# A second norm from three sums, and one uneven load, at the end of a cached attention decode

## The chip, the cores and the metric

The kernel runs on one core of a Trainium2 chip. Its engines are TensorE (PE: matmuls, and PEld: its weight loads), VectorE (DVE), ScalarE (ACT), GpSimd (POOL) and SyncE (SP, which issues nearly all transfers); sixteen DMA engines move the data. The metric is the device time of one execution in microseconds, and the number that counts is the median over the runs. Everything is float32.

## The reference

Batch B = 4, one token each, D = 512; 32 query heads in 8 groups of 4, head size 128, 4096 cached positions; a mixer with F = 1792.

```python
mod = (silu(c) @ w_mod).reshape(4, 6, 1, 512)
sa, ca, ga, sb, cb, gb = (mod[:, i] for i in range(6))
h = layernorm(x) * (1 + ca) + sa
x = x + ga * attention(h, k_cache, v_cache, wq, wo)   # softmax over 4096 positions
h = layernorm(x) * (1 + cb) + sb
# the mixer has a LayerNorm of its own:
n = layernorm(h)                                       # eps 1e-5
x = x + gb * (gelu(n[..., None] * w1 + b1) @ w2 + b2)  # per channel, over F
```

The key and value caches are 4 x 8 x 4096 x 128 each, 134 MB together, and every byte is read once. So a row of the result (one of the batch of four) passes three norms: of x, of the sum x1 after the attention (the first one here), and of h, the modulated first one (the "second norm" of the title).

## The kernel before, in words

**Loads.** A pair i (0 to 31) is one batch row and one key/value group. The data come in slots of 32 KB per partition, three in a ring (pool `ring`, tag `kv`). `load_pair(i)` fills one slot with the keys of pair i+2 (16 KB of each of the 128 rows) and the values of pair i (the other 16 KB). All issues go through SP's queue in program order; an issue waits until PE has read the slot's former content. The last pairs are loaded in pieces (LK, LV, LW in the plan), the last values in pieces down to 128 KB.

**Work on a pair.** `scores` (PE, L231), the row maximum (DVE, L236), its turn and spread over the partitions (L240 to L256), `expo` (ACT, L261), the transposition of p (DVE, L267 or L271), `values` (PE, L291; narrow form L303), a copy (L314), the choice of the four heads (L328), the product with wo (L343) and its addition (L361). For pairs 0 to 23 these steps stand in one loop (line 618). Pairs 24 to 31 follow `PLAN` (line 667), an order written out by hand: each word is one step, and each engine works through its own steps in that order.

**Rows and the mixer.** When the eight pairs of a batch row are done, `Mixer` forms x1, its norm, h and the norm of h, then u = gelu(n w1 + b1) in seven pairs of columns (`expand` on DVE L442, `gelu` on ACT L506) and the contraction with w2 (`contract_wide`, PE L453). Channels stand as four blocks of 128 on the partitions, each value eightfold. Rows 0 to 2 do this beside the loads of later rows. Row 2's last two pairs of columns are contracted (`c c` in the plan) and folded (`zc`, line 520, with fold_groups L366) in the last line of the plan.

**The last row** has nothing left to hide behind. Its products with wo go into `pgx` by L348; `tally_up` (L601) and `mean_last` (L604) give the mean of x1 while they run. Then, in the plan's last line: `zs`, squares of x1 - mean with their sum (ACT L741); `za`, a = (x1 - mean)(1 + cb) (DVE L410); `zx`, a copy of x1 (L747); `zq`, the sum of squares over the row (PE L737), from which `zm` makes the deviation sd (ACT L416), h1 = sb sd + a (DVE L417), an epsilon column (L419) and the statistics of h1 (L378, L380); `zb0` and `zb1`, h1 spread over the partitions (PE L427); `zv`, the statistics gathered (L479); `zn`, the aggregate (DVE L396), the inverse root (POOL L100), two ACT copies of h1 less its mean into hb (L436), and wr = -w1 times the inverse root (POOL L437). `T2` and `T3` load ACT's tables for Sqrt and Gelu. `finish` (line 552) then forms the gelus (ACT L557 twice, L562 five times), the contraction (L447), the products with gb (L567 to L577) and the stores.

Of the kernel before, what the change touches and what calls it, by code (L numbers as in the profile page):

```python
# [8 lines left out]
F32 = mybir.dt.float32  # L9
# [15 lines left out]
NARROW = NS - 3  # L25


@with_exitstack
def adaln_decode(ctx: ExitStack, tc: tile.TileContext, small, x, wmod, wq, kk, kv, vv, wo, out):
# [144 lines left out]
    def load_pair(i):  # L174
        t = slots()
        nc.sync.dma_start(t, kv[i])
        key(t[:, 0], i + 2)
        value(t[:, 1], i)
# [194 lines left out]
    XK = cst.tile([P, B, P], F32, name="xk")  # L373
# [34 lines left out]
    def centre(x, mu):  # L408
        a = wk.tile([P, P], F32, name="a")
        dv.scalar_tensor_tensor(a, x, mu, prep[:, 3], op0=OP.add, op1=OP.mult)  # L410
        return a

    def adaln_last(b, pst, a):
        r = cst.tile([P, 1], F32, name="sd")
        h1 = wk.tile([P, P], F32, name="h1")
        nc.scalar.activation(r, pst, AF.Sqrt, bias=epsc, scale=1.0 / D)  # L416
        dv.scalar_tensor_tensor(h1, prep[:, 2], r, a, op0=OP.mult, op1=OP.add)  # L417
        pst = ps_m.tile([P, 27], F32, name="pst", tag="m")
        dv.tensor_scalar(pst[:, 24:27], eps9, r, r, op0=OP.mult, op1=OP.mult)  # L419
        return h1, stats(h1, b), pst  # L420

# [28 lines left out]
    def contract_wide(py, u, js):  # L450
        for e, j in enumerate(js):
            q = j % 4
            mm(py[32 * q:32 * q + 32, :], w2[:, j:j + 1].to_broadcast([P, 32]), u[:, e, :],  # L453
               start=(j < 4), stop=(j >= NF - 4))

    class Mixer:


        def __init__(self, b):
            self.b, self.wide, self.n = b, b < B - 1, 0  # L460
            self.raw, self.done, self.ripe, self.pbs = [], [], 0, []
            self.pst = None
# [15 lines left out]
        def gather_more(self):  # L478
            mm(self.pst[:, 0:24], ones, self.st.rearrange("p a b -> p (a b)"), start=True, stop=True)  # L479
            self.st = self.pst  # L480

        def modulate(self):
            if self.b < B - 1:
                self.h1, self.st = adaln(self.b, self.st)
            else:
                self.h1, self.st, self.pst = adaln_last(self.b, self.st, self.a)
# [26 lines left out]
        def consume(self, most=9):  # L513
            if self.py is None:
                self.py = ps_e.tile([P, D if self.wide else P], F32, name="py", tag="e")
            for u, js in self.done[:most]:
                (contract_wide if self.wide else contract)(self.py, u, js)
            del self.done[:most]

        def gather_up(self):  # L520
            yw = wk.tile([P, D], F32, name="yw", tag="yw", bufs=1)
            dv.tensor_copy(yw, self.py)
            self.py = fold_groups(ps_e, yw, "e")

# [27 lines left out]
    def finish(b, pg, py, hb, wr):  # L552
        uu = ring.tile([P, 16, D], F32, name="uu", tag="kv")
        for js in ((0,), (1,), (2, 3, 4), (5, 6, 7), (8, 9, 10), (11, 12), (13,)):
            j = js[0]
            if j < 2:
                nc.scalar.activation(uu[:, j], hb, AF.Gelu_apprx_tanh, bias=b1[:, j:j + 1], scale=wr[:, j:j + 1])  # L557
                u = uu[:, j:j + 1]
            else:
                u = uu[:, j:j + len(js)]  # L560
                expand(u, hb, wr, js)
                nc.scalar.activation(u, u, AF.Gelu_apprx_tanh)  # L562
# [5 lines left out]
        dv.tensor_add(osb[:, :B - 1], osb[:, :B - 1], XK[:, :B - 1])  # L568
# [28 lines left out]
    mu = cst.tile([P, 1], F32, name="mu")  # L597

# [19 lines left out]
    for i in range(NS - HKV):  # L618
# [43 lines left out]
    mix, row = Mixer(B - 2), Mixer(B - 1)  # L662
# [11 lines left out]
    v30.1 A29 LW p29 f v30.2 v30.3 t31.0 P29 g V30 Y y a30 A30 p30 E x v31.0 f v31.1 v31.2 v31.3 V31 z31 a31 I A31 j p31  # L674
    g T2 zs za zx zq c c zm zb0 T3 zv zb1 zw0 zn zc
# [5 lines left out]
           "N": mix.normalise, "g": mix.gelu, "c": lambda: mix.consume(1), "zc": mix.gather_up, "zv": row.gather_more,  # L681
           "zg": row.gather,
           "zm": row.modulate, "zn": lambda: row.normalise(cst.tile([P, 1], F32, name="yl"))}
    for step in PLAN.split():
# [49 lines left out]
        elif op == "zq":  # L734
            ph = ps_s.tile([P, 8, P], F32, name="ph3", tag="s")
            row.st = ph[:, 2, 0:1]
            mm(row.st, g32[:, 8 * (B - 1):8 * (B - 1) + 1].to_broadcast([P, P]), sq, start=True, stop=True)  # L737
        elif op == "zs":
            sq = cst.tile([P, 1], F32, name="sq")
            flat = wk.tile([P, P], F32, name="flat")  # L740
            nc.scalar.activation(flat, pgx[:, 4], AF.Square, bias=mu, accum_out=sq)  # L741
        elif op == "j":
            tally_up()
        elif op == "za":
            row.a = centre(pgx[:, 4], mu)
        elif op == "zx":
            dv.tensor_copy(XK[:, B - 1], pgx[:, 4])  # L747
        elif op == "zw":
            modmm(pgx[:, 0], 5, (0,))
        elif op == "zb":  # L750
            if i:
                py = ps_v.tile([P, 4, P], F32, name="py3", tag="pv")
            row.spread(py[:, 2:4] if i else ph[:, 4:6], (2 * i, 2 * i + 1))
    finish(B - 1, pgx[:, 0], py[:, 0], row.hb, row.wr)
# [34 lines left out]
```

## Time and profile before

| what | value |
|---|---|
| runs | 386.43, 386.49, 388.0 us; median 386.49 |
| span of the profiled execution | 384.7 us (no other time is recorded for it; the median of the runs is 1.8 above) |
| DMA queue of SP | 7376 packets, 157.33 MB, 95.4% of sixteen engines' span |
| PE, DVE, ACT, POOL busy | 298.7, 198.2, 112.2, 7.7 us |
| last product into pgx, first gelu of the last row, last store issued: starts | 369.25, 373.88, 382.27 us |

Times in rows of the profile count from the span's start. A row of the timeline gives start and duration, the engine and line, out<-in with shapes, how many instructions are merged, and in brackets the engine's idle time before it with what ended it. The DMA share is the mean busy share of sixteen engines. A transfer has landed when the last of its engines is done.

### The profile page before, as it was taken

The page shows a single profiled execution, that of the slowest core. Times are in us where ns is not written, and L with a number is a line of the kernel's source. Part 1 is how long each engine was busy: PE and PEld are TensorE (multiplying, and loading weights), DVE is VectorE, ACT ScalarE, POOL GpSimd, SP SyncE. Part 2 cuts the span into 40 slices and gives each one's busy share as a digit, 9 for nine tenths or more (in the row PEclk, how much of TensorE's full clock was granted, in tenths as well). Part 3 has the DMA queues.
Part 4 walks back from the last instruction along what each step waited for, and adds up shares of the span by engine and source line. Part 5 has one row for each costly group of instructions (what it writes and reads, how often), then busy time and mean ns, then how long its engine had stood idle before and what let it go on. Part 6 is the DMA issues. An engine that isn't in the chain of part 4 may idle for free.

```text
span 384.7 us, 5604 instructions
## 1 busy us (share of the span) xinstructions
PE 298.7 (78%) x2380; PEld 117.2 (30%) x2380; DVE 198.2 (52%) x407; ACT 112.2 (29%) x144; POOL 7.7 (2%) x33
## 2 busy tenths in 40 slices
PE   0856777866966949979877878788888887999984
PEld 0112122311323313334322222342222343333653
DVE  1130251620451424664866545557665567778757
ACT  1001111121110110212567311124575105657276
POOL 1100000000000000000000000000000000000000
PEclk9989555985695685998999998999999999999999
DMA  8999999999999999999999999999999999999930
GB/s 331 433 433 436 411 453 433 409 432 436 423 441 433 434 436 436 434 436 431 429 425 433 428 433 434 429 433 431 429 434 436 434 436 432 424 417 423 418 122 3
DMA packets 7409, 157.69 MB, mean 410 GB/s; under 512 B 964, under 2 KB 1236, under 8 KB 1496
## 3 DMA queue, kind: packets, MB, share of 16 engines
q1 hardware_dynamic: 7376, 157.33, 95.4%
q8 instruction: 18, 0.29, 0.3%
q14 instruction: 7, 0.06, 0.0%
q10 hardware_dynamic: 8, 0.00, 0.0%
HBM read 157.32 MB, written 0.01 MB: 409 GB/s over the span
## 4 chain that ended last, share of the span: by engine, by line
DMA 60%; PE 29%; DVE 7%; ACT 2%; issue 1%; POOL 0%; SPq 0%; POOLq 0%; DVEq 0%
DMA kv<-in_kv 58%; PE s L231 8%; PE pv L291 7%; PE s L122 2%; PE qs L138 2%; DVE m L236 2%; DVE p L267 2%; DMA sm<-in_small 2%; PE pa L343 2%; PE pt L328 2%; ACT uu L562 1%; PE pb L251 1%; PE pve L303 1%; PE pm L240 1%; PE pgx L348 1%
## 5 line engine op out<-in xcount | busy, mean ns | idle before, releaser
L231 PE MATMUL s<-kv,QT 128*32 128x512 f32 x512 | 75.2, 714 | 38.9 <-DMA kv<-in_kv 37.0
L236 DVE TENSOR_REDUCE m<-s 128x1 f32<-128x1024 f32 x32 | 39.2, 1224 | 96.0 <-PE s L231 95.9
L261 ACT ACTIVATE p<-s,nm 128x1024 f32<-128x1024 f32 x32 | 35.7, 1115 | 180.6 <-DVE nm L256 180.5
L291 PE MATMUL pv<-kv,p 128*32 128x512 f32 x464 | 69.8, 670 | 0.7 <-DMA kv<-in_kv 0.7
L231 PEld LDWEIGHTS s<-kv,QT 128*32 128x32 f32 x512 | 15.8, 123 | 84.0 <-DMA kv<-in_kv 52.5
L328 PEld LDWEIGHTS pt<-g,po 128*128 128x128 f32 x236 | 31.1, 205 | 27.2 <-issue 19.9
L343 PE MATMUL pa<-wo,oT 128*32 128x512 f32 x240 | 34.6, 648 | 4.6 <-DVE oT L335 4.4
L328 PE MATMUL pt<-g,po 128*128 128x4 f32 (+2 forms) x236 | 33.9, 267 | 1.5 <-DVE po L314 1.0
L267 DVE STREAM_TRANSPOSE p<-p 128x1024 f32<-128x1024 f32 x25 | 30.9, 1234 | 0.0
L314 DVE COPY po<-pv 128x512 f32<-128x512 f32 x29 | 20.0, 688 | 16.8 <-PE pv L291 16.7
L245 DVE TENSOR_REDUCE mx<-pm 1x128 f32<-1x512 f32 x32 | 21.3, 669 | 1.1 <-PE pm L240 1.1
L442 DVE TENSOR_SCALAR u<-hb,wr,sm 128x512 f32<-128x512 f32 x40 | 19.9, 541 | 1.9 <-POOL wr L437 1.0
L506 ACT ACTIVATE u<-u 128x1024 f32<-128x1024 f32 x20 | 20.4, 1051 | 1.5 <-DVE u L442 1.4
L361 DVE TENSOR_TENSOR acc<-acc,pa 128x512 f32<-128x512 f32 x26 | 17.8, 686 | 4.3 <-PE pa L343 4.2
L261 ACT ACT_TABLE_LOAD x11 | 14.1, 1283 | 20.3 <-DVE nm L256 20.2
L251 PEld LDWEIGHTS pb<-neg,mx 1*128 1x128 f32 x64 | 10.4, 202 | 28.2 <-DVE mx L245 26.5
L122 PE MATMUL s<-wm,sT 128*4 128x512 f32 x16 | 9.1, 732 | 10.6 <-DVE sT L108 10.6
L506 ACT ACT_TABLE_LOAD x13 | 16.7, 1283 | 0.2
L291 PEld LDWEIGHTS pv<-kv,p 128*32 128x32 f32 x464 | 13.4, 146 | 7.2 <-issue 3.1
L240 PE MATMUL pm<-ident,m 128*1 128x128 f32 x32 | 9.3, 289 | 7.4 <-DVE m L236 3.5
L251 PE MATMUL pb<-neg,mx 1*128 1x1 f32 x64 | 13.1, 271 | 2.1 <-DVE mx L245 2.1
L453 PE MATMUL py<-u,sm 128*32 128x512 f32 x80 | 14.4, 616 | 0.0
(158 smaller groups left out, 214.7 us busy)
## 6 DMA issues: line engine op xcount, KB each, us to landing
kv<-in_kv SPq DMA_DIRECT2D x28, 4096.0 KB, 21.9
wq<-in_wq SPq DMA_DIRECT2D x2, 4096.0 KB, 16.3
wo<-in_wo SPq DMA_DIRECT2D x4, 2048.0 KB
kv<-in_kv SPq DMA_DIRECT2D x4, 2048.0 KB, 20.3
wm<-in_wmod SPq DMA_DIRECT2D x2, 2048.0 KB, 14.8
kv<-in_kk SPq DMA_DIRECT2D x1, 4096.0 KB
kv<-in_vv SPq DMA_DIRECT2D x3, 1024.0 KB
wm<-in_wmod SPq DMA_DIRECT2D x1, 1024.0 KB
```

The costliest lines, as they stand in the source:

```text
L231: mm(s[32 * c:32 * c + 32, n * 512:(n + 1) * 512], QT[:, b, h, :], KT[i][:, (n * 4 + c) * 512:(n * 4 + c + 1) * 512], start=True, stop=True)
L236: dv.tensor_reduce(M[i], S[i], axis=AX.X, op=OP.max)
L245: dv.tensor_reduce(mx, M[i].rearrange("o (c r) -> o r c", c=4).unsqueeze(1).to_broadcast([1, 4, 32, 4]), axis=AX.X, op=OP.max)
L251: mm(pb, M[i].rearrange("o c r -> o (c r)"), neg1, start=True, stop=True)
L261: nc.scalar.activation(p, S[i], AF.Exp, bias=M.pop(i), accum_out=l)
L267: dv.transpose(PL[i][0], PL[i][0])
L291: mm(PV[i][32 * q:32 * q + 32, :], pT[:, 128 * k:128 * k + 128:4], VT[i][:, 4 * k:4 * k + 4, :].rearrange("p j d -> p (j d)"), start=(k < ...
L314: dv.tensor_copy(PV[i], pv)
L328: mm(pt, po[:, c * DH:(c + 1) * DH], sel.unsqueeze(1).to_broadcast([P, m, REP]), start=(c == 0), stop=(c == n - 1))
L343: mm(pa[32 * g:32 * g + 32, :], oT[:, g:g + 1].to_broadcast([P, 32]), wo_t[h][:, g, :], start=True, stop=True)
L442: dv.tensor_scalar(u[:, e, :], hb, wr[:, j:j + 1], b1[:, j:j + 1], op0=OP.mult, op1=OP.add)
L506: nc.scalar.activation(u, u, AF.Gelu_apprx_tanh)
```

## The change

Two edits.

**One uneven load.** `load_pair(16)` becomes four transfers: 24 KB of all 128 rows, and the last 8 KB of rows 0 to 111, 112 to 119 and 120 to 127.

**The second norm from three sums.** With a = (x1 - mean)(1 + cb) and s = sb, h1 = s sd + a up to the common factor 1/sd. The mean and variance of h1 follow from the sum of a, the sum of a squared, the sum of a (s - mean s), the variance of s and sd. What concerns s alone is prepared after pair 5 (`spread_shift`). At the end `centre` takes the sum of a along, `products` the two others, one matmul (`moments`) adds them over the row's partitions, and DVE reads the three sums in PSUM. The variance takes three operations on 128x1, and hb = (s - mean s) sd - mean a + a, with a spread by PE. The epsilon column, h1, its statistics, their gathering, the aggregate, the copies into hb on ACT and the copy of x1 go. Row 2's mixer is folded in another way: its contraction of columns 0 to 9 is copied out early (`zy`, before the last product with wo), and `fold_rest` adds the last four columns block by block onto the fold (`zc0`, `zc1`).

```diff
-    eps9 = cst.tile([P, 3], F32, name="eps9")
-    nc.gpsimd.memset(eps9, 0.0)
-    nc.gpsimd.memset(eps9[:, 0:1], 1e-20)
-    nc.gpsimd.memset(eps9[:, 2:3], EPS * D)
...
+    mine = g32[:, 8 * (B - 1):8 * (B - 1) + 1]
+    mid = cst.tile([P, 1], F32, name="mid")
+    nc.gpsimd.tensor_scalar(mid, mine, 1.0 / D, None, op0=OP.mult)
...
     def load_pair(i):
         t = slots()
-        nc.sync.dma_start(t, kv[i])
+        if i == UNEVEN:
+            main = SK + SK // 2
+            rows, src = t.rearrange("p s n -> p (s n)"), kv[i].rearrange("p s n -> p (s n)")
+            nc.sync.dma_start(rows[:, :main], src[:, :main])
+            for lo, hi in ((0, 112), (112, 120), (120, 128)):
+                nc.sync.dma_start(rows[lo:hi, main:], src[lo:hi, main:])
+        else:
+            nc.sync.dma_start(t, kv[i])
...
-    def contract_wide(py, u, js):
+    def contract_wide(py, u, js, last):
...
-               start=(j < 4), stop=(j >= NF - 4))
+               start=(j < 4), stop=(j > last - 4))
...
+        def lift(self):
+            self.yw = wk.tile([P, D], F32, name="yw", tag="yw", bufs=1)
+            dv.tensor_copy(self.yw, self.py)
+
+        def fold_rest(self, k):
+            if k == 0:
+                self.py = ps_e.tile([P, P], F32, name="pc", tag="e")
+                for c in range(4):
+                    mm(self.py[32 * c:32 * c + 32, :], g32, self.yw[:, c * P:(c + 1) * P], start=True, stop=False)
+            rest = [(u[:, e], j) for u, js in self.done for e, j in enumerate(js)]
+            for u, j in rest[2 * k:2 * k + 2]:
+                for c in range(4):
+                    mm(self.py[32 * c:32 * c + 32, :], w2[:, j:j + 1].to_broadcast([P, 32]),
+                       u[:, c * P:(c + 1) * P], start=False, stop=(j == NF - 1))
...
-        dv.scalar_tensor_tensor(gx, gbl, b2, XK[:, b], op0=OP.mult, op1=OP.add)
+        dv.scalar_tensor_tensor(gx, gbl, b2, x1, op0=OP.mult, op1=OP.add)
...
+    def spread_shift():
+        psb = ps_m.tile([P, 4, P], F32, name="psb", tag="m")
+        for c in range(4):
+            e = 32 * c + 8 * (B - 1)
+            mm(psb[:, c, :], ident[:, e:e + 1].to_broadcast([P, P]), prep[:, 2], start=True, stop=True)
+        nc.scalar.activation(shift, psb.rearrange("p c n -> p (c n)"), AF.Copy)
+        st = wk.tile([P, 6], F32, name="st")
+        dv.bn_stats(st, shift)
+        dv.bn_aggr(smv, st)
+        dv.tensor_scalar(shift, shift, smv[:, 0:1], None, op0=OP.subtract)
+        dv.tensor_scalar(spart, prep[:, 2], smv[:, 0:1], None, op0=OP.subtract)
+        dv.tensor_scalar(smv[:, 1:2], smv[:, 1:2], EPS, None, op0=OP.add)
+
+    def centre(x):
+        a = wk.tile([P, P], F32, name="a")
+        dv.scalar_tensor_tensor(a, x, mu, prep[:, 3], op0=OP.add, op1=OP.mult, accum_out=mom[:, 0:1])
+        return a
+
+    def squares(x):
+        flat = wk.tile([P, P], F32, name="flat")
+        nc.scalar.activation(flat, x, AF.Square, bias=mu, accum_out=sq)
+
+    def products(a):
+        junk = wk.tile([P, P], F32, name="h1")
+        dv.tensor_tensor_reduce(junk, a, a, 1.0, 0.0, OP.mult, OP.add, mom[:, 1:2])
+        dv.tensor_tensor_reduce(junk, a, spart, 2.0, 0.0, OP.mult, OP.add, mom[:, 2:3])
+
+    def spread_centred(ph, a, cs):
+        for c in cs:
+            e = 32 * c + 8 * (B - 1)
+            mm(ph[:, c * P:(c + 1) * P], ident[:, e:e + 1].to_broadcast([P, P]), a, start=True, stop=True)
+
+    def deviation():
+        ps = ps_m.tile([P, 1], F32, name="psq", tag="m")
+        mm(ps, mine.to_broadcast([P, P]), sq, start=True, stop=True)
+        nc.scalar.activation(sd, ps, AF.Sqrt, bias=epsc, scale=1.0 / D)
+
+    def moments():
+        pg = ps_m.tile([P, 3], F32, name="pmo", tag="m")
+        mm(pg, mid.to_broadcast([P, P]), mom, start=True, stop=True)
+        return pg
+
+    def variance(pg):
+        dv.scalar_tensor_tensor(vr[:, 0:1], smv[:, 1:2], sd, pg[:, 2:3], op0=OP.mult, op1=OP.add)
+        dv.scalar_tensor_tensor(vr[:, 1:2], vr[:, 0:1], sd, pg[:, 1:2], op0=OP.mult, op1=OP.add)
+        dv.scalar_tensor_tensor(vr[:, 2:3], pg[:, 0:1], pg[:, 0:1], vr[:, 1:2], op0=OP.mult, op1=OP.subtract,
+                                reverse1=True)
+
+    def affine_last(ph, pg):
...
+        root(vr[:, 2:3], P, y)
+        dv.tensor_scalar(shift, shift, sd, pg[:, 0:1], op0=OP.mult, op1=OP.subtract)
+        dv.tensor_add(hb, shift, ph)
+        nc.gpsimd.tensor_tensor(wr, w1, y.to_broadcast([P, NF]), op=OP.mult)
+        return hb, wr
...
+        if i == 5:
+            spread_shift()
...
-    v30.1 A29 LW p29 f v30.2 v30.3 t31.0 P29 g V30 Y y a30 A30 p30 E x v31.0 f v31.1 v31.2 v31.3 V31 z31 a31 I A31 j p31
-    g T2 zs za zx zq c c zm zb0 T3 zv zb1 zw0 zn zc
+    v30.1 A29 LW p29 f v30.2 v30.3 t31.0 P29 g V30 Y y a30 A30 p30 E x v31.0 f v31.1 v31.2 v31.3 V31 z31 a31 I A31 j zy p31
+    g T2 za zs zr zc0 zq zg zp zm zc1 T3 zn zw0
```

In the plan's new last line, `zr` is `products`, `zg` `moments`, `zp` `spread_centred`, `zm` `variance`, `zn` `affine_last`; `zw0`, a part of the product for gb, now stands last. `finish` reads x1 from `pgx` in PSUM.

More of the change, by code (lines that the diff above doesn't have):

```diff
@@ L25 @@
 NARROW = NS - 3
+UNEVEN = 16
 @with_exitstack
@@ L371, in residual @@
         dv.tensor_add(x1, x1, prep[:, 0])
-    XK = cst.tile([P, B, P], F32, name="xk")
+    XK = cst.tile([P, B - 1, P], F32, name="xk")
     ZK = cst.tile([P, B - 1, P], F32, name="zk")
@@ L406, in adaln @@
         return h1, stats(h1, b)
[L408 to L420, printed above, removed]
     def bcast(h1, b, pb=None, cs=range(4)):
@@ L476, in gather @@
             self.pst = None
-        def gather_more(self):
-            mm(self.pst[:, 0:24], ones, self.st.rearrange("p a b -> p (a b)"), start=True, stop=True)
-            self.st = self.pst
         def modulate(self):
[L483 to L486, printed above, removed]
+            self.h1, self.st = adaln(self.b, self.st)
         def spread(self, pb=None, cs=range(4)):
@@ L550, in outer, with finish @@
                 self.close()
-    def finish(b, pg, py, hb, wr):
+    def finish(b, pg, py, hb, wr, x1):
         uu = ring.tile([P, 16, D], F32, name="uu", tag="kv")
@@ L597, in adaln_decode @@
     mu = cst.tile([P, 1], F32, name="mu")
+    shift = osb.rearrange("p b n -> p (b n)")
+    smv = cst.tile([P, 2], F32, name="smv")
+    spart = cst.tile([P, P], F32, name="spart")
+    mom = cst.tile([P, 3], F32, name="mom")
+    sq = cst.tile([P, 1], F32, name="sq")
+    sd = cst.tile([P, 1], F32, name="sd")
+    vr = cst.tile([P, 3], F32, name="vr")
+    def spread_shift():
[10 more added lines that the diff above has]
+        dv.tensor_scalar(smv[:, 1:2], smv[:, 1:2], EPS, None, op0=OP.add)
@@ new lines, in variance @@
+    def variance(pg):
[4 more added lines that the diff above has]
+    def affine_last(ph, pg):
+        y = cst.tile([P, 1], F32, name="yl")
+        wr = wk.tile([P, NF], F32, name="wr")
+        hb = wk.tile([P, D], F32, name="hb")
+        root(vr[:, 2:3], P, y)
[3 more added lines that the diff above has]
+        return hb, wr
@@ L680, in adaln_decode @@
     MIX = {"F": mix.fold, "R": mix.residual, "G": mix.gather, "M": mix.modulate, "H": mix.gather, "Q": mix.spread,
-           "N": mix.normalise, "g": mix.gelu, "c": lambda: mix.consume(1), "zc": mix.gather_up, "zv": row.gather_more,
-           "zg": row.gather,
-           "zm": row.modulate, "zn": lambda: row.normalise(cst.tile([P, 1], F32, name="yl"))}
+           "N": mix.normalise, "g": mix.gelu, "c": lambda: mix.consume(1), "zy": mix.lift, "zq": deviation}
     for step in PLAN.split():
@@ L733, in adaln_decode @@
             nc.scalar.activation(tab, neg1, AF.Gelu_apprx_tanh)
[L734 to L737, printed above, removed]
+        elif op == "za":
+            al = centre(pgx[:, 4])
         elif op == "zs":
-            sq = cst.tile([P, 1], F32, name="sq")
-            flat = wk.tile([P, P], F32, name="flat")
-            nc.scalar.activation(flat, pgx[:, 4], AF.Square, bias=mu, accum_out=sq)
+            squares(pgx[:, 4])
+        elif op == "zr":
+            products(al)
+        elif op == "zp":
+            ph = ps_s.tile([P, D], F32, name="ph3", tag="s")
+            spread_centred(ph, al, range(4))
+        elif op == "zc":
+            mix.fold_rest(i)
+        elif op == "zg":
+            pg = moments()
+        elif op == "zm":
+            variance(pg)
+        elif op == "zn":
+            hb, wr = affine_last(ph, pg)
         elif op == "j":
             tally_up()
[L744 to L747, printed above, removed]
         elif op == "zw":
             modmm(pgx[:, 0], 5, (0,))
[L750 to L754, printed above, removed]
+    py = ps_v.tile([P, P], F32, name="py3", tag="pv")
+    finish(B - 1, pgx[:, 0], py, hb, wr, pgx[:, 4])
 def kernel(**inputs):
```

10 lines of the change are left out of this document (5 added, 5 removed).

## The prediction

> **What bounds the kernel now.** I read the page first: the span, the slices, the queues, the chain.
>
> ```profile
> span 384.7 us, 5604 instructions
> DMA  8999999999999999999999999999999999999930
> GB/s 331 433 433 436 411 453 433 409 432 436 423 441 433 434 436 436 434 436 431 429 425 433 428 433 434 429 433 431 429 434 436 434 436 432 424 417 423 418 122 3
> q1 hardware_dynamic: 7376, 157.33, 95.4%
> q8 instruction: 18, 0.29, 0.3%
> DMA 60%; PE 29%; DVE 7%; ACT 2%; issue 1%; POOL 0%; SPq 0%; POOLq 0%; DVEq 0%
> ```
>
> The sixteen DMA engines are full until slice 38; 157 MB at some 430 GB/s is the kernel. Only two things can shorten it: the last bytes landing sooner, or less work behind them. The chain of waits says where transfers hand over to compute:
>
> ```profile
> 327.22 15.81 DMA kv<-in_kv
> 343.04 0.14 issue
> 343.17 1.92 PE s L231 x16
> ```
>
> Up to 343.04 us the chain is transfers; from there PE and DVE work through the last pairs, each still fed by a later transfer. So a transfer queue that is early by some amount at 343 moves everything behind it by that amount.
>
> Are the sixteen engines done together? A table by stretch of time (DMA share next to last, GB/s last):
>
> ```profile
> 320.00:340.00 20.00, 18.40 (x133) 7.13 (x129) 15.46 (x36) 10.48 (x13) 0.00 (x0) 0.91 0.99 424
> 366.00:367.00 1.00, 1.00 (x46) 0.97 (x40) 0.88 (x3) 0.69 (x1) 0.00 (x0) 1.00 0.92 354
> 367.00:368.00 1.00, 0.97 (x20) 0.56 (x12) 0.29 (x1) 0.99 (x2) 0.00 (x0) 1.00 0.64 267
> 368.00:369.00 1.00, 1.00 (x19) 0.88 (x22) 0.40 (x3) 0.86 (x2) 0.00 (x0) 1.00 0.56 238
> 369.00:370.00 1.00, 0.87 (x40) 0.60 (x28) 0.16 (x1) 0.06 (x1) 0.00 (x0) 1.00 0.22 82
> ```
>
> They are not. Seven of sixteen finish around 367 (share 0.56 = nine engines left through 368 to 369), the nine others 2 to 3 us later. A transfer counts as landed when its last engine is done, so all of the tail goes by the late nine. Where the lateness comes from, I get by chaining the packet records of the trace, each to the packet that begins as it ends, into sixteen streams (my own grouping; no view prints it). Each 16 KB instruction fetch of the q8 row lies between the data packets of one stream and leaves that stream late for the rest of the run; the fetches go round eight streams, twice. The four-row load of x runs on four streams, and none of these four is ever hit.
>
> The stretch behind the last transfer, from the timeline (start, duration, what, idle before it and its releaser):
>
> ```profile
> 369.25 0.62 PE L348 MATMUL pgx<-wo,both 128*32 128x128 f32 x16
> 369.50 0.16 DVE L607 COPY mu<-pmu 128x1 f32<-128x1 f32 x1 [0.56 <-PE pmu L606]
> 369.94 0.37 ACT L741 ACTIVATE flat<-pgx,mu 128x128 f32<-128x128 f32 x1 [1.07 <-PE pgx L348]
> 370.20 0.19 ACT L741 ACTIVATION_READ_ACCUMULATOR flat<-pgx,mu 128x1 f32 x1
> 370.43 0.35 DVE L410 SCALAR_TENSOR_TENSOR a<-pgx,mu,prep 128x128 f32<-128x128 f32 x1 [0.77 <-ACT flat L741]
> 370.45 0.38 PE L737 MATMUL ph<-sq,g 128*128 128x1 f32 x2 [0.58 <-ACT flat L741]
> 370.87 0.26 ACT L416 ACTIVATE sd<-ph,epsc 128x1 f32<-128x1 f32 x1 [0.47 <-PE ph L737]
> 371.15 1.28 ACT L733 ACT_TABLE_LOAD   x1
> 371.43 0.28 DVE L419 TENSOR_SCALAR pst<-eps,sd 128x3 f32<-128x3 f32 x1
> 371.94 0.18 DVE L380 TENSOR_TENSOR stm<-st,ident 128x24 f32<-128x24 f32 x1
> 372.45 0.69 PE L427 MATMUL py<-h,ident 128*128 128x128 f32 x4
> 372.64 0.28 DVE L396 BATCH_NORM_AGGREGATE mv<-pst 128x2 f32<-128x27 f32 x1 [0.52 <-PE pst L479]
> 372.84 0.63 DVE L522 COPY yw<-py 128x512 f32<-128x512 f32 x1
> 373.00 0.55 POOL L100 TENSOR_TENSOR yl<-mv,half 128x1 f32<-128x1 f32 x1 [54.02 <-DVE mv L396]
> 373.63 0.21 POOL L437 TENSOR_TENSOR wr<-w1n,yl 128x14 f32<-128x14 f32 x1
> 373.88 1.52 ACT L557 ACTIVATE uu<-hb,sm,wr 128x512 f32<-128x512 f32 x2
> ```
>
> From 369.94 (last row's sum done) to 373.88 (first gelu) is 3.94 us in which PE, ACT, DVE and POOL pass small tiles to each other. This is the stretch that the new algebra replaces. Behind 373.88 ACT works without a break through its gelus, and the change leaves that part alone.
>
> **The split pair.** Pair 16 keeps its bytes. Its first 24 KB per row go as before, eight rows an engine. The last 8 KB go as 112 rows (seven an engine) and twice eight rows, which can occupy eight engines at one row each. So eight engines carry 8 KB more than before and eight carry 8 KB less. One engine moves 424/16 = 26.5 GB/s by the row of 320 to 340, so 8 KB is 0.31 us. Which eight get more is not told by the trace of before, which holds no eight-row transfer. Bounds: the never-hit ones, then the late engines gain 0.31; the late ones, then they lose 0.31. The nearest row of its kind is the load of x: four rows, four streams, all unhit. If eight rows continue the choice of four, at least four and probably all eight are unhit, so I take a gain of 0.31, less 0.03 for three more completion records and smaller packets: **0.28 us**. It persists to the end because the queue never runs dry, as the DMA slices show, and it reaches the end in full since both the handover at 343.04 and each later landing move with it.
>
> [...]
>
> Three more issues on SP cost it time, with the loads of pairs 17 and on queued behind them:
>
> ```profile
> SPq L176 <- PE pv L291: 186.4, 23, 12.3
> kv<-in_kv SPq DMA_DIRECT2D x28, 4096.0 KB, 21.9
> ```
>
> SP spends 186.4/23 = 8.1 us on average waiting for a slot before such an issue, and a load is issued 21.9 us ahead of its landing, of which 4096 KB at 430 GB/s is 9.8. Some 12 us of queue hide three issues of about 0.4 us each; without that cover they would cost 1.2.
>
> **The early preparation** (after pair 5): four small products, one ACT copy of 128x512, one statistics pass and four small DVE operations. DVE gets about 2 us: by the rows below 0.68 for the statistics, 0.54 and about 0.35 for the two subtractions, 0.28 and 0.2 for the rest. What hides it is the idle time of that stretch:
>
> ```profile
> 105.00:125.00 20.00, 13.19 (x87) 5.54 (x83) 7.19 (x12) 2.02 (x4) 0.00 (x0) 0.80 1.01 435
> L231 PE MATMUL s<-kv,QT 128*32 128x512 f32 x32 | 5.5, 827 | 6.5 <-DMA kv<-in_kv 6.5
> L113 DVE BATCH_NORM_STATS2 st<-xr x1: 675/675/675, 10.5 to 10.5; 4x6 f32<-4x512 f32 x1
> L442 DVE TENSOR_SCALAR u<-hb,wr,sm 128x512 f32<-128x512 f32 x40 | 19.9, 541 | 1.9 <-POOL wr L437 1.0
> L361 DVE TENSOR_TENSOR acc<-acc,pa 128x512 f32<-128x512 f32 x26 | 17.8, 686 | 4.3 <-PE pa L343 4.2
> 364.90 0.35 DVE L726 CUSTOM_DVE_ANT_0 ep<-ep,prep,g 128x128 f32<-128x128 f32 x1
> 365.17 0.08 DVE L726 DVE_READ_ACCUMULATOR2_ANT tally<- 128x1 f32 x1
> 376.92 0.86 PE L447 MATMUL py<-uu,sm 128*32 128x128 f32 x24 [0.39 <-ACT uu L562]
> ```
>
> DVE is 7.19 of 20 us busy there and PE waits 6.5 us for transfers, so it costs nothing; uncovered, 2 us. The three memsets that go and the one POOL operation (1/512 of the mask) that comes lie in the first microseconds. POOL's mask waits for DVE's folding of the identity, and the silu of c stands behind it; the first two weight transfers, issued already, cover that.
>
> **The new tail, step by step.** Readers of one PSUM tile take turns: DVE's L410 stood 0.77 us until ACT's L741 was done, though both only read pgx. Now DVE goes first.
> - centre with its sum: 369.94, 0.35 and an accumulator read. By L726 the pair ends 0.36 after its start: 370.30.
> - ACT's squares behind it, 0.45 as before with their accumulator (369.94 to 370.39): 370.34 to 370.80. From there to the deviation the same hops as before, 370.39 to 371.13 = 0.74: sd at **371.54**, where it was 371.13.
> - DVE's two products, 0.36 each with 0.04 between and ahead: 371.10. The product with mid, and back to DVE, like L380's end (372.12) to L396 (372.64) = 0.52: moments at **371.62**. PE has the deviation product ahead of it in its queue, which is through by 371.2.
> - variance: three dependent operations on 128x1. No such row; L607 at 0.16 and L419 at 0.28 are the bounds. I take 0.22, as they have two scalars like the larger: with 0.04 between, 371.62 + 0.74 = **372.36** (372.18 to 372.54).
> - POOL: mv's end (372.92) to the gelu (373.88) was 0.96 with the power and the product for wr. So wr allows 373.32.
> - DVE: shift scaled, 0.54 (L442; its PSUM scalar could make it 0.69 as in L361), then the sum with PSUM, 0.69 (L361): 372.40 + 0.54 + 0.04 + 0.69 + 0.04 = **373.71**. This ends last, and the first gelu goes from 373.88 to 373.71.
>
> So the tail gains **0.17** us (bounds: 0.35 gained with the short variance, 0.15 lost with the long one and the slow shift). The removed operations (x1 copied, h1, its statistics, the aggregate, two ACT copies for hb) are in the difference of the two ends. What is added beside the path: the first fold, 24 PE instructions, 0.86 by L447, from 369.87 to 370.73 in a gap in which PE waited for ACT, ahead of the deviation product at 370.85; the cover is 0.1, and uncovered it costs what it exceeds that. The spread, 2 x 0.7 by L427, ends at 372.6 before the sum needs it at 372.98. The second fold and the gate's product run while PE waits for the first gelu. The lift, 0.63 as L522, moves ahead of mu on DVE: from 368.94 it ends at 369.57 and pushes mu to about 369.75, still before pgx at 369.94. It costs nothing by 0.2 us. ACT's table load follows sd and ends by 373.1, before the gelu.
>
> **Sum.** 0.28 + 0.17 = 0.45 us off the profiled execution's span of 384.7. The three runs were 386.43, 388.0 and 386.49, so the median is 1.8 above that span; I take the same distance after: 386.49 - 0.45 = **386.0**.
>
> **The rivals.**
> - The split moves nothing, since the engines' finishing order differs or the engines are levelled anyway: 386.49 - 0.17 = 386.3. For it: PE is also nearly full from 360 to 367. Against it: nine engines at work through 368 to 369. [...]
> - The eight-row pieces fall on the late engines. Place: every landing after pair 16; price +0.31; it decides as soon as one of the latest streams is among the eight. 386.49 + 0.31 - 0.17 = 386.6, slower. Against it: the four rows of x.
> - DVE becomes the bound of the tail. From sd on it has five dependent operations where before it had two or three on the path. If each 128x1 costs 0.35 like the 128x128 of L410 and each hand-over 0.1, variance takes 1.35 instead of 0.74, and shift and sum wait 0.06 more each: 0.73 later than forecast, 386.8. It decides when the variance exceeds 0.74 + 0.45.
> - The change does not do what it says: the early preparation holds a slot so long that a transfer starts late. Price 2 us at most, 388; the queue of 12 us speaks against it.
>
> **How the numbers follow.** Forecast 0.55; split without effect 0.2; DVE as bound 0.1; pieces on late engines 0.08; early disturbance 0.04; a larger gain 0.03. The likeliest gives 386.0. The range takes in 0.31 + 0.35 gained at one end, with the runs' scatter beyond, and at the other the late pieces or the slow DVE, alone or together: 385.2 to 387.2. A change of under 0.5% (1.9 us) is about what a measurement here cannot tell from none. Every case but the early disturbance stays within it, and the third run before shows that a run can lie 1.5 above: faster 0.03, same 0.92, slower 0.05.
>
> **What would show it.** The handover from transfers to PE at 342.76 where it is 343.04; the DMA share nearer to level between 367 and 369 (the early seven 0.3 later, the others 0.3 earlier); wait of DVE for ACT at pgx gone and ACT's squares starting at 370.3 relative to pgx at 369.9; sum into hb ending last before the first gelu, 3.77 us after pgx, with wr ready 0.4 before it. It is wrong if the handover does not move or moves later, if wr or the variance ends last, or if the deviation product waits for the first fold.

## The result: slower by 0.9%

| | before | after |
|---|---|---|
| median (us) | 386.49 | 390.41 (389.72 to 390.56) |
| ratio, 95% interval | | 1.009 (1.0066 to 1.0114) |
| span of the profiled execution | 384.7 | 388.6 |

The forecast was 386.0 in a range of 385.2 to 387.2. The kernel lost 3.9 us instead, and its time lies outside the range. Single runs, of the kernel before too, lie 1 to 5 us above the others of their kernel; the ratios follow the means of the runs and take such runs in, the medians hardly move with them. The page of the kernel after:

```profile
span 388.6 us, 5679 instructions
DMA  8999999999999999999999999999999999999920
GB/s 328 432 432 432 423 438 432 425 434 432 427 435 432 430 435 435 430 432 430 436 437 433 422 304 428 432 430 435 432 430 432 430 428 435 422 430 425 414 104 3
q1 hardware_dynamic: 7536, 157.33, 95.3%
DMA 66%; PE 22%; DVE 6%; ACT 3%; issue 1%; POOL 0%; SPq 0%; POOLq 0%; ACTq 0%
```

The bytes are the same 157.33 MB, and the DMA engines count as full to the end. But one slice, the twenty-fourth (223.4 to 233.2 us), moved 304 GB/s where before it moved 433. One slice is 9.7 us, so the missing 126 GB/s are 1.2 MB, which at 430 GB/s take 2.8 us; its neighbour (422) adds a little. This is where pair 16's pieces are loaded. A busy share of 9 in that slice says only that packets were under way, not that they moved at full rate.

A table by stretch (its length, then busy time of PE, PEld, DVE, ACT and POOL with their instructions, the granted clock, the DMA share, GB/s) places it. The kernel after:

```profile
215.00:222.00 7.00, 5.12 (x51) 1.59 (x51) 3.46 (x8) 1.20 (x2) 0.00 (x0) 1.00 1.01 434
222.00:226.00 4.00, 3.64 (x35) 1.69 (x31) 2.97 (x5) 0.00 (x0) 0.00 (x0) 1.00 0.97 408
226.00:230.00 4.00, 2.33 (x22) 0.61 (x20) 1.64 (x4) 1.21 (x2) 0.00 (x0) 1.00 1.07 264
230.00:234.00 4.00, 3.79 (x34) 1.68 (x34) 2.09 (x3) 0.00 (x0) 0.00 (x0) 1.00 1.06 301
234.00:238.00 4.00, 3.15 (x31) 0.99 (x27) 3.20 (x10) 1.21 (x2) 0.00 (x0) 1.00 0.97 414
```

and the kernel before, at the place of the dip:

```profile
226.00:230.00 4.00, 2.01 (x18) 0.51 (x10) 1.40 (x3) 1.21 (x2) 0.00 (x0) 0.98 1.08 467
230.00:234.00 4.00, 3.53 (x19) 0.93 (x20) 0.19 (x1) 0.00 (x0) 0.00 (x0) 0.60 0.91 393
```

For 8 us the rate is 264 to 301 GB/s, where the kernel before moves 430 on average, while the share is above 1. A row counts a packet, with all its time and bytes, where the packet begins, so that a share can come out above 1: it is 1.08 in the kernel before as well, at 467 GB/s, and tells nothing of the rate. The packet times below show that the packets last longer here (531 ns at the median for 8 KB, against 309). At 430 GB/s these 8 us would have moved 3.44 MB; they moved 2.26. The difference, 1.18 MB, is 2.7 us; the two neighbouring rows, 408 and 414, add 0.4. That is 3.1 of the 3.9 us; where the rest goes, these rows don't tell.

It is never made good. The chain of waits of the kernel after (start, duration, what):

```profile
322.29 0.14 issue
322.43 1.39 PE pv L298 x8
...
351.25 18.91 DMA kv<-in_vv
370.16 0.04 issue
370.20 1.35 PE pve L310 x28
```

Before, the chain left the transfers for good at 343.04. Now it goes through the engines from 322.43 on, comes back to a transfer at 351.25 and stays with it to 370.16, so that late transfers bound the last pairs too. By the semaphore records of the trace (no view prints them singly) the last value piece lands at 371.41, where before it landed at 367.53: 3.9 us later.

### The profile page after: what moved, and what is told of

Its sections match the earlier page's. It is cut to its first block, busy times and chain, and to the rows that moved or that the text cites. A ratio compares the mean times of both kernels' runs of the same rounds, so it can differ in the third digit from the quotient of the medians.

```text
span 388.6 us, 5679 instructions
## 1 busy us (share of the span) xinstructions
PE 291.6 (75%) x2412; PEld 115.8 (30%) x2412; DVE 200.6 (52%) x416; ACT 112.0 (29%) x143; POOL 8.0 (2%) x31
## 3 DMA queue, kind: packets, MB, share of 16 engines
q1 hardware_dynamic: 7536, 157.33, 95.3%
## 4 chain that ended last, share of the span: by engine, by line
DMA 66%; PE 22%; DVE 6%; ACT 3%; issue 1%; POOL 0%; SPq 0%; POOLq 0%; ACTq 0%
DMA kv<-in_kv 55%; PE s L238 7%; PE pv L298 6%; DMA kv<-in_vv 5%; DMA kv<-in_kk 4%; DVE m L243 3%; PE s L122 2%; DVE p L274 2%; DMA sm<-in_small 2%; ACT uu L563 1%; PE pt L335 1%; PE pa L350 1%; PE pb L258 1%; PE pm L247 1%; DVE mx L252 0%
## 5 line engine op out<-in xcount | busy, mean ns | idle before, releaser
L238 PE MATMUL s<-kv,QT 128*32 128x512 f32 x512 | 74.1, 703 | 47.6 <-DMA kv<-in_kv 46.8
L298 PE MATMUL pv<-kv,p 128*32 128x512 f32 x464 | 66.6, 641 | 1.3 <-DMA kv<-in_kv 1.3
L335 PEld LDWEIGHTS pt<-g,po 128*128 128x128 f32 x236 | 29.8, 197 | 27.1 <-issue 20.6
L350 PE MATMUL pa<-wo,oT 128*32 128x512 f32 x240 | 32.8, 618 | 5.1 <-DVE oT L342 4.8
L335 PE MATMUL pt<-g,po 128*128 128x4 f32 (+2 forms) x236 | 32.5, 262 | 1.5 <-DVE po L321 1.0
L247 PEld LDWEIGHTS pm<-ident,m 128*1 128x1 f32 x32 | 2.5, 79 | 34.8 <-DVE rl L287 25.0
```

The costliest lines, as they stand in the source:

```text
L238: mm(s[32 * c:32 * c + 32, n * 512:(n + 1) * 512], QT[:, b, h, :], KT[i][:, (n * 4 + c) * 512:(n * 4 + c + 1) * 512], start=True, stop=True)
L298: mm(PV[i][32 * q:32 * q + 32, :], pT[:, 128 * k:128 * k + 128:4], VT[i][:, 4 * k:4 * k + 4, :].rearrange("p j d -> p (j d)"), start=(k < ...
L335: mm(pt, po[:, c * DH:(c + 1) * DH], sel.unsqueeze(1).to_broadcast([P, m, REP]), start=(c == 0), stop=(c == n - 1))
L350: mm(pa[32 * g:32 * g + 32, :], oT[:, g:g + 1].to_broadcast([P, 32]), wo_t[h][:, g, :], start=True, stop=True)
```

## The experiments

Each kernel was run beside the kernel before, whose median in these runs was 386.45 to 386.53. The line numbers of its rows are those of that kernel.

### Which of the two edits: algebra_only and split_only

algebra_only is the kernel after without the uneven load; split_only is the kernel before with it.

```diff
# algebra_only, against after
-UNEVEN = 16
+UNEVEN = -1
# split_only, against before
-        nc.sync.dma_start(t, kv[i])
+        if i == 16:
+            main = SK + SK // 2
...
+            nc.sync.dma_start(rows[:, :main], src[:, :main])
+            for lo, hi in ((0, 112), (112, 120), (120, 128)):
+                nc.sync.dma_start(rows[lo:hi, main:], src[lo:hi, main:])
+        else:
+            nc.sync.dma_start(t, kv[i])
```

> The changed kernel with pair 16 loaded in one transfer again; the new tail and the early preparation stay. Theory A (the row and column split of pair 16 costs all of the loss): 386.2, that is 0.24 us below the kernel before, since from the last product into pgx to the first gelu the changed kernel took 3.70 us (373.81 to 377.51) and the one before 3.94 (369.94 to 373.88); the DMA rate has no slice under 400 GB/s between 40 and 360 us. Rival (the early preparation or the new tail costs it): 388 to 390.

> The kernel before with nothing changed but pair 16's load in four transfers (24 KB of all rows, then 8 KB of 112, 8 and 8 rows). Theory A: 390.4 to 390.7, the loss of the changed kernel and the tail's gain of 0.24 missing; the DMA rate falls to about 260 to 300 GB/s for some 8 us where pair 16 lands. Rival (the split costs nothing alone and the loss comes of the early preparation or the tail): 386.2 to 386.8.

Measured: algebra_only 386.28 (386.11 to 387.57), ratio 0.9997 (0.9988 to 1.0006). split_only 390.23 (390.05 to 390.35), ratio 1.0096 (1.008 to 1.0111). The whole loss is the split load; the early preparation and the new tail cost nothing that can be measured, and gain nothing that can be measured either. The page of algebra_only has no dip:

```profile
span 384.4 us, 5674 instructions
GB/s 331 433 436 436 411 457 430 406 439 426 430 442 430 435 436 436 431 436 435 431 435 426 415 433 435 426 438 433 436 435 436 435 429 430 423 420 426 416 133 3
```

and split_only, with the tail of before, has the one of the kernel after (by stretch):

```profile
226.00:230.00 4.00, 2.11 (x18) 0.51 (x10) 1.50 (x4) 1.20 (x2) 0.00 (x0) 1.00 1.07 250
230.00:234.00 4.00, 3.74 (x34) 1.76 (x34) 1.96 (x3) 0.00 (x0) 0.00 (x0) 1.00 1.05 303
```

### Cut by columns or by rows: columns_only and rows_only

The split has two cuts: 24 KB and 8 KB of each row, and 112, 8 and 8 rows. columns_only keeps the first alone, rows_only the second alone, with all 32 KB of a row in each piece.

```diff
# columns_only, against split_only
-            for lo, hi in ((0, 112), (112, 120), (120, 128)):
-                nc.sync.dma_start(rows[lo:hi, main:], src[lo:hi, main:])
+            nc.sync.dma_start(rows[:, main:], src[:, main:])
# rows_only, against split_only
-            main = SK + SK // 2
...
-            nc.sync.dma_start(rows[:, :main], src[:, :main])
...
-                nc.sync.dma_start(rows[lo:hi, main:], src[lo:hi, main:])
+                nc.sync.dma_start(rows[lo:hi, :], src[lo:hi, :])
```

> The kernel before, pair 16 as two transfers of all 128 rows: the first 24 KB of each row, then the last 8 KB. Theory R (it is the cut by rows: engines that carry 7 or 1 rows in a run meet on the way into the same partitions): no loss, 386.4 to 386.6, and the 8 KB pieces move at 430 GB/s. Theory C (it is the cut by columns: 8 KB pieces out of rows that lie 32 KB apart are slow to read): 8 rows an engine at 0.53 us in place of 0.31, that is about 1.8 us lost, 388.3.

> The kernel before, pair 16 in whole rows of 32 KB as 112, 8 and 8 rows, no cut by columns. [...] Theory C: no loss by the cut; the eight engines with two rows more end 32 KB or 1.2 us later and, where they are the late ones, cost that: 386.5 to 387.7.

Measured, one run each: columns_only 386.7, rows_only 400.81. The time of columns_only lies within the runs of the kernel before in this set (386.32 to 386.75): smaller packets and another issue cost nothing that shows. The cut by rows costs 14.4 us with 4 MB in it, and 3.8 us with 1 MB: four times the bytes, 3.8 times the loss. So the loss goes with the bytes that travel in the row-cut form, some 3.6 to 3.8 us for each MB, and not with the number of transfers, which is one less in rows_only.

The stretch of pair 16 in columns_only:

```profile
226.00:230.00 4.00, 3.94 (x36) 1.06 (x28) 1.34 (x3) 1.21 (x2) 0.00 (x0) 1.00 1.10 471
230.00:234.00 4.00, 3.64 (x29) 1.69 (x29) 3.76 (x6) 0.00 (x0) 0.00 (x0) 1.00 0.95 410
```

and in rows_only, in steps of 10 us:

```profile
220.00:230.00 10.00, 6.96 (x58) 2.56 (x53) 4.84 (x9) 1.21 (x2) 0.00 (x0) 1.00 0.99 252
230.00:240.00 10.00, 0.00 (x0) 0.00 (x0) 0.12 (x1) 0.00 (x0) 0.00 (x0) 0.55 1.14 197
240.00:250.00 10.00, 4.86 (x30) 2.04 (x34) 1.54 (x3) 0.00 (x0) 0.00 (x0) 0.60 0.86 311
```

In the second row PE does nothing for 10 us: the stall is plain in the compute engines when the bytes are many. In the trace's packet records (no view prints them singly), an 8 KB packet of pair 16 takes 309 ns in columns_only, and at the median 560 ns in split_only and 531 in the kernel after. The packets of the 128-row transfers that run beside them grow too: those of 24 KB, 0.91 us in columns_only, take up to 1.8 us in split_only, and those of 32 KB, 1.21 us elsewhere, up to 2.5. So packets of the usual work are held up as well.

### What in the row cut: sixteens, halves, 112 and 16

Four kernels keep the 24 KB transfer of pair 16 and cut the rows of the last 8 KB in other ways:

```diff
# sixteens_next: rows 0 to 63, then 64 to 79, 80 to 95, 96 to 111, 112 to 127
# sixteens_apart: rows 0 to 63, then 64, 68, ... 124; 65, 69, ...; 66, ...; 67, ...
# halves_64: rows 0 to 63, then 64 to 127
# even_112_16, against split_only
-            for lo, hi in ((0, 112), (112, 120), (120, 128)):
+            for lo, hi in ((0, 112), (112, 128)):
```

> The kernel before, pair 16's last 8 KB as rows 0 to 63 and then rows 64 to 79, 80 to 95, 96 to 111, 112 to 127: sixteen engines with one row each, sixteen neighbouring rows at a time. [...] Rival R2 (each further transfer, or each transfer of fewer than 128 rows, costs a fixed time): the same loss in both twins. Rival R3 (only the odd counts, seven rows an engine or eight engines, are slow): no loss in either, 386.5.

> The twin: the same five transfers of the same 8 KB, but rows 64, 68, ... 124, then 65, 69, ... and so on, sixteen rows that are four apart. [...] R2: as the twin. R3: no loss.

> The kernel before, pair 16's last 8 KB as rows 0 to 63 and rows 64 to 127, four rows an engine. [...] R3 (odd counts alone are slow): 386.5. [...]

> The kernel before, pair 16's last 8 KB as rows 0 to 111 and rows 112 to 127 (one row an engine), so that every engine carries the same bytes. [...] If unequal bytes per engine were the cause: 386.5.

Measured:

| kernel | median us (range) | ratio (95%) |
|---|---|---|
| sixteens_next | 390.57 (390.3 to 390.84) | 1.0093 (1.0058 to 1.0128) |
| sixteens_apart | 390.15 (389.62 to 391.05) | 1.0083 (1.0047 to 1.0119) |
| halves_64 | 390.31 (389.85 to 390.7) | 1.007 (1.0023 to 1.0117) |
| even_112_16 | 390.02 (389.63 to 391.44) | 1.0059 (1.0013 to 1.0105) |

All four lose 3.5 to 4.1 us, as the split itself does. By the forecast's count of rows over sixteen engines, even_112_16 and halves_64 give every engine the same bytes, and they hold no eight-row piece: neither the unequal load nor the eight-row pieces are the cause. even_112_16 keeps the 112 rows and loses 3.5, but halves_64, which has no such piece, loses 3.8. The twin sixteens, one with neighbouring rows and one with rows four apart, are 0.4 apart, inside their scatter. The dip looks alike too; halves_64, then even_112_16:

```profile
226.00:230.00 4.00, 2.08 (x22) 0.67 (x18) 1.24 (x3) 1.20 (x2) 0.00 (x0) 1.00 1.11 268
230.00:234.00 4.00, 3.79 (x34) 1.61 (x26) 2.24 (x3) 0.00 (x0) 0.00 (x0) 1.00 0.96 274
```

```profile
226.00:230.00 4.00, 2.24 (x22) 0.54 (x14) 1.61 (x4) 1.21 (x2) 0.00 (x0) 1.00 1.12 268
```

Two theories were left. Either any transfer of fewer than 128 rows is slow in itself (R2 in the expectations below), or what counts is which rows an engine writes (R1): by this theory each engine has eight rows of its own in a transfer of 128 rows, and an engine that is sent to the rows of another meets that engine there. R1 is an assumption of the author's: no trace here shows which engine writes which row.

### Fewer rows, or foreign rows: the four extra loads

For this the kernel before gets a transfer that it never reads, issued at about 60 us and moved at 80 to 86, into the last 8 KB per row of the ring slot that the modulation's third weights leave empty. extra_128 adds it for all 128 rows (1 MB). The three others add 256 KB: 32 rows in four transfers of eight, so that the bytes, the number and size of the transfers and, by the packet counts, the number of engines (eight) are the same. In the kernel after, each eight-row transfer of pair 16 leaves eight landing records, and those of 112 and 128 rows sixteen (semaphore records; no view prints them singly). extra_own and extra_next even read and write the same rows; only which rows go together in a transfer differs.

```diff
# all four, against before
-        w = ring.tile([P, 3, 4, D], F32, name="wm24", tag="kv")
+        flat = slots().rearrange("p s n -> p (s n)")
+        w = flat[:, :12 * D].rearrange("p (e k n) -> p e k n", e=3, k=4)
+        spare, src = flat[:, 12 * D:], kv[16].rearrange("p s n -> p (s n)")[:, 12 * D:]
...
# extra_128
+        nc.sync.dma_start(spare, src)
# extra_own: rows 0 to 31, each transfer takes rows four apart
+        for j in range(4):
+            nc.sync.dma_start(spare[j:32:4], src[j:32:4])
# extra_next: rows 0 to 31, each transfer takes eight neighbours
+        for j in range(0, 32, 8):
+            nc.sync.dma_start(spare[j:j + 8], src[j:j + 8])
# extra_other: rows 64 to 95, each transfer takes rows four apart
+        for j in range(64, 68):
+            nc.sync.dma_start(spare[j:96:4], src[j:96:4])
```

> The kernel before with one transfer more, never read: behind the three modulation weights (about 60 us) 8 KB of all 128 rows go into the 8 KB of that slot that nothing uses. It measures what 1 MB costs in the full form. All theories: 1 MB at 430 GB/s, 2.4 us; 388.9.

> The same place, 8 KB of rows 0 to 31 only, in four transfers of eight rows that are four apart (0, 4, ... 28; 1, 5, ... 29; and so on). 256 KB, all on the eight engines that an eight-row transfer takes, four rows or 1.2 us each. Theory R1 (an engine that writes rows of another engine's share meets that engine there; an engine on its own rows meets nobody): each engine stays on its own rows; if these eight are the early ones, their lead of 1.5 to 2.5 us takes it and nothing is lost, 386.5; if they are the late ones, 1.2 lost, 387.7. Theory R2 (any transfer of fewer than 128 rows runs slow, whichever rows): 3.8 us lost per MB on top, about 1 us, 387.5 or more.

> The same 256 KB, the same eight engines, four rows each, but eight neighbouring rows at a time (0 to 7, 8 to 15, ...). [...] R2: as its twin with rows four apart.

> [...] R2: as its twin on rows 0 to 31.

Measured:

| kernel | median us (range) | ratio (95%) | added |
|---|---|---|---|
| extra_128 (1 MB) | 389.09 (388.89 to 389.13) | 1.006 (1.0041 to 1.008) | 2.56 |
| extra_own (256 KB) | 387.7 (seven runs 387.43 to 387.71, three 389.66 to 392.28) | 1.0056 (1.0023 to 1.0088) | 1.17 |
| extra_next (256 KB) | 390.44 (389.25 to 391.61) | 1.0106 (1.0075 to 1.0137) | 3.91 |
| extra_other (256 KB) | 389.89 (389.7 to 391.43) | 1.0091 (1.0064 to 1.0118) | 3.36 |

The added time is that of the medians. The stretch from 82 to 88 us, first the kernel before, then extra_128, then extra_own, extra_next, extra_other (one fence each):

```profile
82.00:88.00 6.00, 4.06 (x24) 0.56 (x24) 0.00 (x0) 1.09 (x3) 0.00 (x0) 0.59 1.10 474
```

```profile
82.00:88.00 6.00, 3.65 (x24) 0.56 (x24) 0.00 (x0) 1.37 (x3) 0.00 (x0) 0.70 1.11 474
```

```profile
82.00:88.00 6.00, 3.95 (x24) 0.56 (x24) 0.00 (x0) 1.14 (x3) 0.00 (x0) 0.60 1.11 474
```

```profile
82.00:88.00 6.00, 3.23 (x36) 0.79 (x40) 0.00 (x0) 1.75 (x4) 0.00 (x0) 1.00 1.09 369
```

```profile
82.00:88.00 6.00, 3.66 (x24) 0.56 (x24) 0.00 (x0) 1.46 (x3) 0.00 (x0) 0.67 1.08 332
```

extra_own moves at the rate of the 128-row transfer and of the kernel before, 474 GB/s; the two others at 369 and 332. Its 1.17 us are what the bytes alone cost, by an estimate of four rows of 8 KB at 0.31 us on each of eight engines, 1.24 in all. The eight-row transfers of the two others cost 3.91 and 3.36. The intervals of the three ratios overlap, because of extra_own's three late runs, so that the times alone don't settle it; the profiles do, with 474 GB/s at the place against 369 and 332. In bytes the two dips are 0.63 and 0.85 MB, or 1.5 and 2.0 us at 430 GB/s, somewhat less than the 2.2 to 2.7 us between the medians. The profiled runs took 387.61, 389.25 (the fastest of extra_next) and 391.43 us (the slowest of extra_other), so that 369 and 332 are not to be ranked. By the theory that any transfer of few rows is slow, all three were to be alike; it falls, and which rows a transfer takes decides here. R1 agrees with that, but the runs show the rows alone, not the engines that write them. In the packet records of extra_own all packets here last what they last elsewhere (309 ns for 8 KB, 1.21 us for 32 KB); in extra_next and extra_other packets of 32 KB last up to 2.2 and 2.3 us.

R1's picture of two engines that meet at the same rows is not shown to cover all of extra_next: in a grouping of its packets into sixteen streams (each packet chained to the one that begins as it ends; no view prints it), the 32 KB packets of the eight streams that carried no piece take up to 2.0 us too.

## Why the prediction was wrong, step by step

**The split pair, forecast to gain 0.28: it lost 3.8 (split_only).** This is the step that failed. It priced the pieces by bytes per engine at the engine's full rate, 26.5 GB/s, and took for granted that the rate holds whichever rows a transfer takes. split_only against columns_only, and extra_own against extra_next and extra_other, show that it doesn't: in pair 16 the row cut costs 3.5 to 4.1 us for its MB, in the extra loads eight neighbouring rows, or rows 64 to 95, cost 2.2 to 2.7 us more for 256 KB than rows four apart of 0 to 31, by the medians, and the packets of the 128-row transfers beside them are held up too. The bounds of the step, 0.31 either way, came from the same assumption, so the range could not hold the time. No row of the trace before showed a full-rate transfer cut by rows; the forecast said that it holds no eight-row transfer, and then bounded the cost by the load of x, four rows of 2 KB, too small to show a rate.

Its second premise fell as well. The eight rows were to go to engines that the instruction fetches never hit. extra_own's 1.17 us say so: had its 1.24 us of extra bytes fallen on early engines alone, which finish 2 to 3 us before the others, the end would hardly have moved. In a grouping of its packets into streams the eight that carried the eight-row pieces include the last stream of all, which ends some 4 us behind the fastest; over the whole run such a grouping is not certain, since streams in step can be taken for each other. The same holds for the forecast's account of which streams the fetches made late; and that none of the four streams of x is ever hit does not come out of such groupings, in which some of the four carry fetches as well. Even at the full rate the split would then have loaded late engines and lost, by the forecast's own rival, 0.31.

**Three more issues on SP, forecast at nothing: nothing speaks against it.** columns_only has one of the three and took 386.7; extra_own has four and costs its bytes alone. even_112_16, with two instead of three, does not lose less beyond its scatter.

**What would have shown it.** The handover was to move from 343.04 to 342.76; the chain is now with a transfer until 370.16. The finish was to be nearer to level; its shares fall much as before (0.64, 0.56, 0.22 from 367), only later:

```profile
370.00:371.00 1.00, 0.91 (x28) 0.53 (x24) 0.32 (x2) 0.99 (x2) 0.00 (x0) 1.00 0.68 279
371.00:372.00 1.00, 1.00 (x17) 0.63 (x9) 0.29 (x1) 1.00 (x1) 0.00 (x0) 1.00 0.54 229
372.00:373.00 1.00, 1.00 (x22) 0.88 (x25) 0.58 (x4) 0.30 (x2) 0.00 (x0) 1.00 0.33 131
```

**The early preparation, forecast at nothing: right.** The kernel after, same stretch as the forecast's cover:

```profile
105.00:125.00 20.00, 11.90 (x88) 4.37 (x84) 7.44 (x13) 1.21 (x2) 0.00 (x0) 0.83 1.01 434
```

DVE is 7.44 of 20 us busy, and the rate is 434 GB/s as before (435). algebra_only's 386.28 agrees.

**The new tail, forecast to gain 0.17: gained 0.24.** The timeline of the kernel after, from the centring on:

```profile
373.81 0.35 DVE L623 SCALAR_TENSOR_TENSOR a<-pgx,mu,prep 128x128 f32<-128x128 f32 x1 [0.28 <-PE pgx L355]
374.21 0.37 ACT L628 ACTIVATE flat<-pgx,mu 128x128 f32<-128x128 f32 x1 [1.90 <-DVE a L623]
374.54 0.29 DVE L633 CUSTOM_DVE_ANT_0 h<-a,spart 128x128 f32<-128x128 f32 x1
374.72 0.38 PE L642 MATMUL psq<-sq,g 128*128 128x1 f32 x2 [0.32 <-ACT flat L628]
375.14 0.26 ACT L643 ACTIVATE sd<-psq,epsc 128x1 f32<-128x1 f32 x1 [0.47 <-PE psq L642]
375.45 0.22 DVE L651 SCALAR_TENSOR_TENSOR vr<-smv,sd,pmo 128x1 f32<-128x1 f32 x1 [0.61 <-ACT sd L643]
375.70 0.21 DVE L652 SCALAR_TENSOR_TENSOR vr<-vr,sd,pmo 128x1 f32<-128x1 f32 x1
375.95 0.22 DVE L653 SCALAR_TENSOR_TENSOR vr<-pmo,vr 128x1 f32<-128x1 f32 x1
376.09 0.54 DVE L661 TENSOR_SCALAR osb<-osb,sd,pmo 128x512 f32<-128x512 f32 x1
376.25 0.79 POOL L100 TENSOR_TENSOR yl<-vr,half 128x1 f32<-128x1 f32 x1 [54.59 <-DVE vr L653]
376.74 0.69 DVE L662 TENSOR_TENSOR hb<-osb,ph 128x512 f32<-128x512 f32 x1
377.12 0.21 POOL L663 TENSOR_TENSOR wr<-sm,yl 128x14 f32<-128x14 f32 x1
377.51 1.52 ACT L558 ACTIVATE uu<-hb,sm,wr 128x512 f32<-128x512 f32 x2 [0.59 <-POOL wr L663]
```

From the centring to the first gelu it takes 377.51 - 373.81 = 3.70 us, where the old tail took 3.94. algebra_only has the same 3.70 (369.88 to 373.58), and split_only, with the old tail, the same 3.94 (373.53 to 377.47): the term is a property of the tail, not of a run. Three times 0.22 for the variance, 0.54 and 0.69 for shift and sum, and the deviation ready 1.59 after the start (forecast 1.60) came out as taken. The deviation product did not wait for the first fold; its row (L642) names ACT's squares. Two sizes were off. The products took 0.29 instead of 0.36, so that the first variance operation waited for the deviation, not for the moments. And the shift, which uses no result of the variance, began 2.28 after the centring, where the forecast had 2.46; two hand-overs behind it took 0.11 of these 0.18 back. That is the 0.07 more. POOL's inverse root, taken as in the tail before (0.55), took 0.79, with DVE at a 128x512 operation beside it at that time; so wr ends at 377.33 and hb at 377.43, where the forecast had 0.4 between them. hb ends last, as forecast, but ACT's row names POOL's wr as what it waited for, and 0.1 is too little to say which of the two decides. That the gain is near the forecast is in part luck: with a root slower by another 0.1, wr would have ended last.

This gain cannot be told from nothing in the times of the runs: algebra_only against before is 0.9988 to 1.0006. It is read from the timeline alone. In the kernel after the sum is: last landing +3.9, tail -0.24, so that the first gelu starts 3.63 later (373.88 to 377.51); the 0.3 that is left up to the span's 3.9 lies behind the issue of the last store (382.27 before, 385.91 after, 3.64 later).

**What stays open.** Why the loss per MB is the same for every row cut of pair 16, and two to three times as large in the extra loads. The engines run out of step: the sixteen landing records of the last load before (L192) come from 366.75 to 370.07, over 3.3 us. That this mixes the pieces is argued, not shown. How one engine's packets lengthen another's is not shown either. Nor was a cut of pair 16 tried in the form of extra_own; that the choice of rows is the cause there too is inferred from the extra loads, and sixteens_apart, with sixteen rows four apart, lost 3.7 all the same. Of the extra loads, extra_own costs its bytes alone but adds them only to eight engines, late ones among them by its time, so that a levelling without loss is not shown to be possible here. The best of these kernels is algebra_only, and it is not to be told from the kernel before.

## What to carry to other kernels

Before you move bytes from one DMA engine to another by cutting a transfer by rows, measure that cut, with the very rows that its pieces take. At the full rate of this kernel, eight-row pieces of rows four apart, of 0 to 31, cost their bytes alone (1.17 us for 256 KB), and pieces of eight neighbours there, or of rows 64 to 95, cost 2.2 to 2.7 us more, far above the 0.3 us that the levelling could gain; the transfers beside them slowed too (32 KB packets up to 2.3 us, elsewhere 1.21). A cut by columns cost nothing that one run shows (386.7). When the trace holds no row for an operation, a bound that takes the known rate for granted is no bound: the range has to hold the case in which the rate itself fails.

## What was not expected of the hardware

- 1 MB loaded in the 128-row form costs 2.56 us when it is added; the same MB, cut by rows, costs 3.5 to 4.1 us more than in that form, whether into 64 and 64, 112 and 16, 112, 8 and 8, or 64 and four times 16.
- With eight-row transfers of rows four apart under way, all loads together moved 474 GB/s when the rows were 0 to 31, and 332 when they were 64 to 95 (in a run that was the slowest of four).
- A slow stretch can show a DMA share above 1 (1.07 at 264 GB/s), and so can a fast one (1.08 at 467): the share of busy time told nothing of the rate here, and the row of GB/s has to be read beside it.
- POOL's power on 128x1 took 0.79 us beside a 128x512 DVE operation, and 0.55 in the tail before, although a 128x512 copy out of PSUM ran on DVE beside most of it; algebra_only shows 0.79 again and split_only 0.55. The cause was not tested.
